# Neighbouring PSUM columns for the dense products, and transposed weight rows kept in their own slab, in a decode kernel with its backward pass

## Chip, cores and metric

One core of one Trainium2 chip. The metric is the device time of one execution in microseconds (us), median over repeated runs.

## The reference

Two layers, each an attention over a given key/value cache and a feed-forward block with squared ReLU, applied twice with the same weights to one token; then the vector-Jacobian product for one output gradient. So the kernel returns the output and the gradients of x, of both caches, and of all weights and biases. Cut to what matters:

```python
# D = 1024, 32 query heads, 4 KV heads, head size 128, cache of 65536 keys, F = 3584, all bf16
def A(x, k_cache, v_cache, wq, wo):
    q = heads(x @ wq)
    p = softmax(q @ k.T * 128 ** -0.5)          # 8 query heads share one KV head
    return merge(p @ v) @ wo

def B(x, w1, b1, w2, b2):
    r = relu(x @ w1 + b1)
    return (r * r) @ w2 + b2

x1 = x  + A(ln(x));   x2 = x1 + B(ln(x1))
x3 = x2 + A(ln(x2));  x4 = x3 + B(ln(x3))       # x4 is the output
# reference: x4 and jax.vjp(...)(grad_out)
```

## The kernel before

It makes four passes over K and V: forward of the first attention, forward of the second, backward of the second, backward of the first. Between the passes lie three "turns", chains of dense matrix-vector products: first turn wo, w1, w2, wq; second turn wo and w1 forward, w1 and wo backward; third turn wq, w2, w1 and wo backward. Products that hang on no vector of the chain run beside it while their slabs are there: w2 with the output's gradient beside the first turn's w2, and x4's own w2 product beside the third turn's. A pass is limited by its transfers; a turn is a chain of vectors, each needed by the next product.

A product whose weights are stored the right way round goes through `g_mv`: each 128x128 block is TensorE's stationary operand, and the vector's chunk is repeated over `rep` columns (64 for eight blocks, 18 for w1's 28).

```python
    def g_mv(slab_it, nk, nbk, xcol, ps_of, finish, side=None, pre=None, cols=d_cols):
        rep = 1 if ps_of is ps_bg else min(64, 512 // nbk)
        ps = ps_of([P, rep, nbk])
        ...
        for kc, slab in slab_it:
            for nb in range(nbk):
                nc.tensor.matmul(ps[:, :, nb], lhsT=cols(slab, nb), rhs=xcol(kc).to_broadcast([P, rep]), ...)
            ...
        finish(ps[:, 0, :])
```

A product with the transposed matrix goes through `Rows`. Each part (up to eight 128x128 blocks of a row of weights) is either multiplied and reduced on VectorE, or transposed on TensorE (`front`), copied from PSUM to a buffer `wt` on ScalarE or VectorE, and multiplied (`back`).

```python
        def front(self, job, kc, slab):
            ...                                   # VectorE multiply-reduce, if the balance model says so
                pt = self.ps_wt()
                for i in range(w):
                    nc.tensor.transpose(pt[:, i, :], job["cols"](slab, k0 + i), ident_b[:, :])
                ...
                wt = self.pool.tile([P, 8, P], BF, name="wt", tag="wt", bufs=self.bufs)
                evac(wt[:, 0:w, :], pt[:, 0:w, :])
                self.queue.append((job, kc, q, wt))
                if len(self.queue) >= self.bufs:
                    yield

    rows = Rows(DENSE["pool"])                    # third turn
    rows.add(PRE["wq3"], DC, R, lambda: L3["dqT"][:, gsl(lastg[2])], fin_dx2)
    def side_x4(kc, slab):
        for nb in range(DC):
            nc.tensor.matmul(ps_x4[:, :, nb], lhsT=d_cols(slab, nb), rhs=L4["gb"]..., ...)
        if kc == FC - 1:
            ...                                   # x4 = x3 + ps_x4 + b2 on VectorE
            col_to_dram(x4, D, out_0...)          # a TensorE transpose, a copy, a store
    rows.add(w2_slabs()[0], FC, DC, lambda: dx2[:], fin_dh2, mix=True, side=side_x4)
    rows.add(w1_slabs()[0], DC, FC, lambda: dh2[:], fin_dx1, cols=f_cols, mix=True)
    rows.add(wo_slabs(firstg[3])[0], R, DC, lambda: dx1[:], dO_finish(L1, firstg[3]))
    rows.run()
```

Names used below: a slab is a piece of a matrix loaded at once, a slot the memory that it takes; dqT is the last gradient of q of a pass, with which the third turn starts; dn3 and dx2 come of the wq product, dh2 of w2's, dx1 of w1's; dO (dOT in the traces) starts the next backward pass. A kc is a band of 128 rows of a matrix (28 of them in w2, four to a slab of 1 MB).

## Time and profile before

| | before |
|---|---|
| median of 3 runs | 2031.34 us (2030.72 to 2031.52) |
| span of the profiled run | 2027.6 us, mean granted TensorE clock 0.904 |
| moved by the transfers | 794.98 MB, mean 392 GB/s |
| busy: TensorE, VectorE, ScalarE | 80%, 58%, 52% of the span |

TensorE is the busiest engine on the page, and that share says little: in the passes it is busy beside transfers that run at their limit. What counts is where the transfers fall below 420 GB/s. The prediction shows these lines.

### The profile page before, as it was taken

The numbers are of one execution on the slowest core, as the hardware profiler recorded it, in microseconds if no ns is written. First come the engines' busy times: TensorE is split into PE (matmuls) and PEld (weight loads), VectorE is DVE, ScalarE is ACT, GpSimd is POOL, SyncE is SP. The second block draws the span as 40 slices with busy tenths as digits, with TensorE's granted clock in tenths as the row PEclk, the third lists the DMA queues.
The fourth block names the chain that finished last, engine by engine and source line by source line (L and its number), as shares of the span: only waits on it lengthen the run. The fifth ranks groups of instructions, "written<-read, shape, count | busy, mean of one in ns | idle before, by whom it ended". The sixth has DMA issues, their size and how long they took to land. (4 is left out here: it accounts for less than half of the span.)

```text
span 2027.6 us, 67015 instructions
## 1 busy us (share of the span) xinstructions
PE 1626.9 (80%) x30210; PEld 1332.9 (66%) x30210; DVE 1174.3 (58%) x2358; ACT 1044.6 (52%) x1613; POOL 144.5 (7%) x332
## 2 busy tenths in 40 slices
PE   6877888687877877787787887788788888698896
PEld 6877777687777776786676885455455555355554
DVE  5645455245554543544454457677667777577675
ACT  3434344144344352435363445587667667577675
POOL 0000000000000000000000001112121111111111
PEclk9989899799999987898998989889888889798888
DMA  9999999989999997899999977999999999999996
GB/s 389 420 420 420 419 423 397 371 362 420 420 418 420 420 399 279 352 420 421 420 417 412 401 267 266 370 410 423 422 420 421 393 423 396 363 402 423 421 379 245
DMA packets 110846, 794.98 MB, mean 392 GB/s; under 512 B 9425, under 2 KB 9439, under 8 KB 49375
## 3 DMA queue, kind: packets, MB, share of 16 engines
q1 hardware_dynamic: 86510, 624.99, 75.7%
q0 software_dynamic: 24048, 165.70, 19.8%
q8 instruction: 236, 3.87, 0.8%
q14 instruction: 52, 0.42, 0.1%
HBM read 624.96 MB, written 165.69 MB: 390 GB/s over the span
## 5 line engine op out<-in xcount | busy, mean ns | idle before, releaser
L153 DVE COPY kt<-ps_tr 128x1024 bf16<-128x1024 bf16 x724 | 497.8, 689 | 473.8 <-PE ps_tr L913 256.7
L150 ACT CAST arena<-ps_gg 128x1024 bf16<-128x1024 f32 x452 | 439.9, 1009 | 219.0 <-PE ps_gg L1280 160.7
L913 PE MATMUL ps_tr<-ident_b,arena 128*128 128x128 bf16 x3840 | 310.2, 226 | 60.4 <-DMA arena<-in_A_k_cache_dram 45.1
L913 PEld LDWEIGHTS <-arena 128*128 128x128 bf16 x3840 | 234.0, 101 | 66.6 <-DMA arena<-in_A_k_cache_dram 48.1
L153 DVE CAST arena<-ps_gg 128x1024 bf16<-128x1024 f32 (+1 forms) x191 | 228.9, 1198 | 82.4 <-PE ps_gg L1280 48.0
L150 ACT COPY kt<-ps_tr 128x1024 bf16<-128x1024 bf16 x164 | 172.2, 1054 | 183.9 <-PE ps_tr L1105 126.0
L1280 PE MATMUL ps_gg<-GG,xt 64*128 64x512 bf16 x1024 | 211.6, 413 | 46.4 <-DVE arena L153 26.8
L1015 PE MATMUL ps_acc<-arena 128*128 128x64 bf16 (+4 forms) x4096 | 206.0, 196 | 45.7 <-DMA arena<-in_A_v_cache_dram 31.7
L1226 PE MATMUL ps_tr<-ident_b,arena 128*128 128x128 bf16 x1824 | 175.9, 234 | 35.3 <-DMA arena<-in_A_v_cache_dram 34.4
L931 PE MATMUL ps_sc<-L_qpad,kt 128*128 128x64 bf16 (+7 forms) x3584 | 183.4, 194 | 17.9 <-issue 11.5
L996 ACT ACTIVATE arena<-S_sb,L_negm 128x128 bf16<-128x128 f32 x256 | 165.4, 1002 | 57.8 <-DVE L_negm L981 57.7
L1105 PE MATMUL ps_tr<-ident_b,arena 128*128 128x128 bf16 x1920 | 156.3, 228 | 48.3 <-DMA arena<-in_A_v_cache_dram 48.3
L1015 PEld LDWEIGHTS <-arena 128*128 128x128 bf16 x4096 | 159.8, 100 | 50.0 <-DMA arena<-in_A_v_cache_dram 34.8
L1226 PEld LDWEIGHTS <-arena 128*128 128x128 bf16 x1824 | 119.5, 104 | 88.8 <-issue 49.6
L931 PEld LDWEIGHTS <-kt 128*128 128x128 bf16 x3584 | 153.3, 100 | 23.6 <-issue 14.6
L1105 PEld LDWEIGHTS <-arena 128*128 128x128 bf16 x1920 | 118.6, 102 | 52.2 <-DMA arena<-in_A_v_cache_dram 51.0
L1306 PE MATMUL ps_acc<-X,arena 128*128 128x64 bf16 (+3 forms) x2048 | 119.7, 199 | 24.8 <-DMA arena<-in_A_k_cache_dram 24.8
L996 ACT ACTIVATION_READ_ACCUMULATOR arena<-S_sb,L_negm 128x1 f32 x256 | 127.8, 499 | 0.0
L1306 PEld LDWEIGHTS <-arena 128*128 128x128 bf16 x2048 | 87.1, 102 | 59.9 <-issue 33.1
L1150 PE MATMUL ps_acc<-dsT,arena 128*128 128x64 bf16 (+7 forms) x2048 | 103.7, 195 | 20.0 <-DMA arena<-in_A_k_cache_dram 15.8
L1280 PEld LDWEIGHTS <-xt 64*128 64x128 bf16 x1024 | 61.3, 94 | 86.3 <-issue 46.8
L1259 PE MATMUL ps_sc<-DOB,kt 128*128 128x64 bf16 (+3 forms) x1824 | 117.5, 200 | 0.0
(266 smaller groups left out, 2169.3 us busy)
## 6 DMA issues: line engine op xcount, KB each, us to landing
arena<-in_A_k_cache_dram SPq DMA_DIRECT2D x86, 2048.0 KB, 21.5
arena<-in_A_v_cache_dram SPq DMA_DIRECT2D x83, 2048.0 KB, 21.4
out_dram<-arena POOLq DMA_DIRECT2D x151, 1024.0 KB, 11.4
arena<-in_A_v_cache_dram SPq DMA_DIRECT2D x76, 1024.0 KB, 16.5
arena<-in_A_k_cache_dram SPq DMA_DIRECT2D x76, 1024.0 KB, 16.8
arena<-in_B_w_dram SPq DMA_DIRECT2D x32, 896.0 KB, 5.8
arena<-in_A_wq_dram SPq DMA_DIRECT2D x22, 1024.0 KB, 13.8
arena<-in_A_wo_dram SPq DMA_DIRECT2D x18, 1024.0 KB, 17.5
```

Source lines behind the costliest of these rows:

```text
L150: nc.scalar.copy(out=out, in_=in_)
L153: nc.vector.tensor_copy(out=out, in_=in_)
L913: nc.tensor.transpose(pt[:, i, :], kb8[:, i, :], ident_b[:, :])
L931: nc.tensor.matmul(state["ps_s"][:, s:s + w, :].rearrange("p a b -> p (a b)"), lhsT=kt[:, i, :], rhs=L["qpad"][:, g, 0:w, :].rearrange("p ...
L996: nc.scalar.activation(out=E(p, g, c0, SU)[:, :, h], in_=S[:, h, :], func=ACTF.Exp, bias=L["negm"][:, g, su, h:h + 1], scale=SCALE, accum_ ...
L1015: nc.tensor.matmul(ps_o[:, 0:w, :], lhsT=vb8[:, i, :], rhs=E(p, g, c, w), start=(c % SU == 0), stop=(c % SU == SU - 1), skip_group_check=True)
L1105: nc.tensor.transpose(pt[:, i, :], vb8[:, i, :], ident_b[:, :])
L1150: nc.tensor.matmul(ps_dq[:, 0:w, :].rearrange("p a b -> p (a b)"), lhsT=kb8[:, i, :], rhs=dsT[:, s:s + w, :].rearrange("p a b -> p (a b)") ...
L1226: nc.tensor.transpose(pt[:, i, :], vb8[:, i, :], ident_b[:, :])
L1259: nc.tensor.matmul(state["ps_dp"][:, s:s + w, :].rearrange("p a b -> p (a b)"), lhsT=vt[:, i, :], rhs=DOB[:, g, 0:w, :].rearrange("p a b - ...
L1280: nc.tensor.matmul(pg[:, 512 * h:512 * h + 512], lhsT=xt[64 * h:64 * h + 64, j1 // 8 + m, :], rhs=gg[64 * h:64 * h + 64, :, :].rearrange(" ...
L1306: nc.tensor.matmul(ps_dq[:, 0:w, :].rearrange("p a b -> p (a b)"), lhsT=kb8[:, i, :], rhs=X[:, s:s + w, :].rearrange("p a b -> p (a b)"), ...
```

## The change

Its intent: (1) PSUM columns of a product lie next to each other, (block, repeat) in place of (repeat, block); (2) wq's and wo's transposed parts are copied back into the slab that they came from, so that all eight parts can be ready before their vector arrives, in memory that needs no buffer; a slab is then freed by its last product, not by its last transpose. The diff, cut to its core:

```diff
-        ps = ps_of([P, rep, nbk])
+        ps = ps_of([P, nbk, rep])
-                nc.tensor.matmul(ps[:, :, nb], lhsT=cols(slab, nb), ...
+                nc.tensor.matmul(ps[:, nb, :], lhsT=cols(slab, nb), ...
-        finish(ps[:, 0, :])
+        finish(ps[:, :, 0])
 # Rows.front
-                if self.views:
+                sl = NOW["slab"]
+                if job["inplace"]:
+                    wt = slab[:, k0 * P:(k0 + w) * P].rearrange("p (a b) -> p a b", b=P)
+                elif self.views:
 ...
-                self.queue.append((job, kc, q, wt))
-                if len(self.queue) >= self.bufs:
+                self.queue.append((job, kc, q, wt, sl))
+                if job["inplace"]:
+                    sl.users += 1
+                else:
+                    self.parts += 1
+                if self.parts >= self.bufs:
 # Rows.back: an in-place part gives its slab up after its products; slabs() frees a slab with no users left
+            if job["inplace"]:
+                sl.users -= 1
+                if sl.over and not sl.users:
+                    sl.free()
 # Rows.run: all parts of a first in-place job go ahead of the rest
+            first = self.queue[0][0] if self.queue else None
+            while first is not None and first["inplace"] and self.queue and self.queue[0][0] is first:
+                self.back()
 # second turn (wo) and third turn (wq, wo)
-    rows.add(PRE["wq3"], DC, R, lambda: L3["dqT"][:, gsl(lastg[2])], fin_dx2)
-    ps_x4 = ps_acc([P, 64, DC])
+    rows.add(PRE["wq3"], DC, R, lambda: L3["dqT"][:, gsl(lastg[2])], fin_dx2, inplace=True)
+    ps_x4 = ps_acc([P, DC, 64])
-            nc.tensor.matmul(ps_x4[:, :, nb], ...
+            nc.tensor.matmul(ps_x4[:, nb, :], ...
-    rows.add(wo_slabs(firstg[3])[0], R, DC, lambda: dx1[:], dO_finish(L1, firstg[3]))
+    rows.add(wo_slabs(firstg[3])[0], R, DC, lambda: dx1[:], dO_finish(L1, firstg[3]), inplace=True)
```

More of the change, by code (lines that the diff above doesn't have):

```diff
@@ L289, in __init__ @@
             self.n = 2 if both else 1
+            self.users, self.over = 0, False
             self.t = wide(self.i) if both else GRAN[self.i]
@@ L432, in gen @@
                 for kk in range(kn):
+                    NOW["slab"] = sl
                     yield k + kk, v[:, kk, :]
-                sl.free()
+                sl.over = True
+                if not sl.users:
+                    sl.free()
         g = gen()
@@ L472, in g_mv @@
                 last = (kc == nk - 1) and (nb == nbk - 1)
-                nc.tensor.matmul(ps[:, :, nb], lhsT=cols(slab, nb), rhs=xcol(kc).to_broadcast([P, rep]),
+                nc.tensor.matmul(ps[:, nb, :], lhsT=cols(slab, nb), rhs=xcol(kc).to_broadcast([P, rep]),
                                  start=first, stop=last, skip_group_check=True)
@@ L567, in __init__ @@
             self.n = 0
+            self.parts = 0
             if pool is None:
@@ L576, in __init__, with add @@
             self.feed = None
-        def add(self, slab_it, nk, nj, vcol, finish, cols=d_cols, mix=False, side=None):
+        def add(self, slab_it, nk, nj, vcol, finish, cols=d_cols, mix=False, side=None, inplace=False):
             job = self.job(nk, nj, vcol, finish, cols, mix)
             job["side"] = side
+            job["inplace"] = inplace
             self.jobs.append((slab_it, job))
@@ L585, in job @@
             pieces = [(k, min(8, nj - k)) for k in range(0, nj, 8)]
-            return dict(side=None, nk=nk, pieces=pieces, nj=nj, vcol=vcol, finish=finish, done=0, cols=cols, mix=mix, vbc=vbc, slot=None)
+            return dict(side=None, inplace=False, nk=nk, pieces=pieces, nj=nj, vcol=vcol, finish=finish, done=0, cols=cols, mix=mix, vbc=vbc, slot=None)
         def begin(self, job):
@@ L649, in back @@
         def back(self):
-            job, kc, q, wt = self.queue.popleft()
+            job, kc, q, wt, sl = self.queue.popleft()
             k0, w = job["pieces"][q]
@@ L658, in back @@
                                  start=(i == 0), stop=(i == w - 1), skip_group_check=True)
+            if job["inplace"]:
+                sl.users -= 1
+                if sl.over and not sl.users:
+                    sl.free()
+            else:
+                self.parts -= 1
             self.did(job)
@@ L692, in fill @@
                 self.feed = self.fronts()
-            while len(self.queue) < self.bufs and next(self.feed, "end") != "end":
+            while self.parts < self.bufs and next(self.feed, "end") != "end":
                 pass
         def run(self):
+            self.fill()
+            first = self.queue[0][0] if self.queue else None
+            while first is not None and first["inplace"] and self.queue and self.queue[0][0] is first:
+                self.back()
             self.fill()
@@ L1508 @@
     rows.add(w1_slabs()[0], DC, FC, lambda: dh4[:], fin_dx3, cols=f_cols, mix=True)
-    rows.add(wo_slabs(firstg[2])[0], R, DC, lambda: dx3[:], dO_finish(L3, firstg[2]))
+    rows.add(wo_slabs(firstg[2])[0], R, DC, lambda: dx3[:], dO_finish(L3, firstg[2]), inplace=True)
     run(g_w1(L4, ps_mv, pre=rows.fill))
@@ L1546 @@
     rows = Rows(DENSE["pool"])
-    rows.add(PRE["wq3"], DC, R, lambda: L3["dqT"][:, gsl(lastg[2])], fin_dx2)
+    rows.add(PRE["wq3"], DC, R, lambda: L3["dqT"][:, gsl(lastg[2])], fin_dx2, inplace=True)
     x4 = vec.tile([P, DC], F32, name="x4")
-    ps_x4 = ps_acc([P, 64, DC])
+    ps_x4 = ps_acc([P, DC, 64])
     def side_x4(kc, slab):
         for nb in range(DC):
-            nc.tensor.matmul(ps_x4[:, :, nb], lhsT=d_cols(slab, nb), rhs=L4["gb"][:, kc:kc + 1].to_broadcast([P, 64]),
+            nc.tensor.matmul(ps_x4[:, nb, :], lhsT=d_cols(slab, nb), rhs=L4["gb"][:, kc:kc + 1].to_broadcast([P, 64]),
                              start=kc == 0 and nb == 0, stop=kc == FC - 1 and nb == DC - 1, skip_group_check=True)
@@ L1557, in side_x4 @@
             f = tmp.tile([P, DC], F32, name="ffn_f")
-            nc.vector.tensor_tensor(out=f[:], in0=ps_x4[:, 0, :], in1=b2c[:], op=ALU.add)
+            nc.vector.tensor_tensor(out=f[:], in0=ps_x4[:, :, 0], in1=b2c[:], op=ALU.add)
             nc.vector.tensor_tensor(out=x4[:], in0=x3[:], in1=f[:], op=ALU.add)
```

## The prediction

> **What bounds the kernel now.** I read the page first, and on it the slices of the span. The kernel makes four passes over a K and a V cache, and between them three "turns" of dense products (wo, w1, w2, wq).
>
> ```profile
> DMA  9999999989999997899999977999999999999996
> GB/s 389 420 420 420 419 423 397 371 362 420 420 418 420 420 399 279 352 420 421 420 417 412 401 267 266 370 410 423 422 420 421 393 423 396 363 402 423 421 379 245
> ```
>
> A slice is 50.7 us. Inside the passes the transfers run at 420 GB/s. The dips at slices 8 and 9, 16 and 17, and 24 to 26 are the three turns. 794.98 MB at 420 GB/s is 1893 us; the other 135 us are start, turns and tail. Compute in a pass is hidden, so only a shorter dip gains time. I then took the sums by stretch around the turns, in steps of 50 us and of 5 us.
>
> ```profile
> core 0: us, PE busy (x) PEld busy (x) DVE busy (x) ACT busy (x) POOL busy (x), PEclk, DMA share, GB/s
> 400.00:405.00 5.00, 4.62 (x89) 4.44 (x88) 5.00 (x10) 2.08 (x3) 0.00 (x0) 1.00 1.00 413
> ...
> 425.00:430.00 5.00, 4.51 (x117) 4.39 (x115) 0.36 (x2) 0.03 (x1) 0.00 (x0) 1.00 0.10 39
> ...
> 1190.00:1195.00 5.00, 5.00 (x110) 5.00 (x108) 4.85 (x9) 3.27 (x5) 0.00 (x0) 1.00 0.37 110
> ```
>
> Summing (420 - rate)/420 x 5 us over the 5 us rows, the idle transfer time is 12.6 us in the first turn (375 to 435 us), 25.1 us in the second (765 to 850) and 36.3 us in the third (1160 to 1260). In a dip the DMA queue waits for slots that the dense chain frees, so what shortens that chain shortens the dip, until the transfers are saturated again.
>
> Then the groups by shape, for the price of one dense product:
>
> ```profile
> L656 PE MATMUL ps_bg<-vcb,wt 128*128 128x64 bf16 x768 | 38.5, 197 | 6.6 <-ACT wt L150 5.2 <-DVE wt L153 0.8 <-DVE vcb L509 0.2
> L473 PE MATMUL ps_mv<-L_gb,arena 128*128 128x64 bf16 x224 | 16.6, 252 | 1.8 <-DMA arena<-in_B_w_dram 1.8
> L1553 PE MATMUL ps_acc<-L_gb,arena 128*128 128x64 bf16 x224 | 15.8, 248 | 0.0
> ```
>
> All three multiply a 128x128 block by one vector repeated over 64 columns. L656 writes neighbouring columns; L473 and L1553 write every eighth fp32. The duration contains a fixed latency, so I took the step between matmuls from the timeline:
>
> ```profile
> 369.92 1.89 PE L1015 MATMUL ps_acc<-arena 128*128 128x64 bf16 x32 [5.96 <-DMA arena<-in_A_v_cache_dram]
> 376.05 6.58 PE L473 MATMUL ps_mv<-L_oTb,arena 128*128 128x64 bf16 x64 [0.71 <-DVE L_oTb L1052]
> 778.47 4.81 PE L473 MATMUL ps_mv<-L_nb,arena 128*128 128x18 bf16 x140 [1.11 <-DVE L_nb L219]
> 423.68 3.73 PE L473 MATMUL ps_mv<-L_nb,arena 128*128 128x64 bf16 x64 [1.11 <-DVE L_nb L219]
> ```
>
> At half clock (0.50 to 0.54 granted there) neighbouring columns cost 1.8/32 = 55 ns and strided ones 6.58/64 = 103 ns. At full clock strided is 3.73/64 = 58 ns, and runs of 8 neighbouring matmuls take 0.40 to 0.44 us, 29 to 33 ns a step. The 18-column product of w1 steps at 34 ns whatever the clock or stride: another floor.
>
> Last, the wait around the third turn's first vector:
>
> ```profile
> 1173.93 0.17 DVE L1083 SCALAR_TENSOR_TENSOR L_dqT<-dqa,L_rZ 128x8 f32<-128x8 f32 x1
> 1174.19 1.01 ACT L150 COPY wt<-ps_tr 128x1024 bf16<-128x1024 bf16 x1 [13.57 <-DVE L_dqT L1083]
> 1186.02 0.15 DVE L878 TENSOR_TENSOR dn<-dn,ps_bg 128x8 f32<-128x8 f32 x1
> ```
>
> wq3's transposes sat in PSUM, but ScalarE idled 13.57 us before copying them out, until dqT was done. A copy needs no dqT: I read this as the wt buffers lying in memory that pass 3 still used (its pool closes with its last vector). From dqT to the wq product's first use is 11.9 us.
>
> **What the Trainium skill says.** "PSUM — Partial Sum Buffer", Specifications (TRN2), gives "8-byte (any non-contiguous AP slows matmuls significantly)"; the trace agrees, a factor of 1.8 to 1.9. "TensorE: Matmul & The Clock Gate", Back-to-back issue gap, gives N/1.2 ns cold and N/2.4 + 2.5 warm, 53 and 29 ns at 64 columns; the trace has 55 and 29 to 33 for neighbouring columns[...]. "HBM Reference", Specifications (TRN2), says a core streaming alone reaches about 425 GB/s; here 420, so passes have no room.
>
> **The change, part by part.** The layout turns the accumulator from (repeat, block) to (block, repeat); operands and counts stay. It touches 64 matmuls each of the first q, wo1, q3 and wo3, 224 of w2 forward and 224 of the side product x4. Their finish reads 8 values 256 bytes apart, which is nothing.
>
> *First turn.* wo1: 64 x (103 - 55) = 3.1 us, all on the path, with w1 and its loads waiting behind it. w2 forward ran from 395.3 to 420.1 us with PE at 4.5 to 5.0 us of every 5: it is PE-bound, and 224 x (58 - 30) = 6.3 us goes. But DVE was full there until 414.2, its multiply-reduces back to back from 395.4: 18.8 us, and w2's last slab landed at 411.7. Shifted by 3.1 these floors are 411.1 and 408.6 plus about 2 us of work; so w2 ends near 411.3, 8.8 us earlier. q3: 64 x (58 - 30) = 1.8 us. The chain is 10.6 us shorter. The transfers, though, have only 12.6 us of idle to give back, and part of it (375 to 390 us) only shifts: I count 9.5.
>
> *Second turn.* wo3, at half clock: 3.1 us. w1 behind it waits for slabs whose slots wo3 frees, so it all moves along. w1's rows are unchanged. In-place wo: its last two parts were transposed and copied after the vector; from vector to dO took 821.5 to 824.6 = 3.1 us, and 64 matmuls at 33 ns are 2.1: 0.9 us. Sum 4.
>
> *Third turn.* wq3: all eight parts can be copied into their own slab before dqT, in idle time. 24 transposes (2.2 us of PE) leave the path. x4: 224 x 28 ns = 6.3 us, somewhat more for the cold ones. PE was fully busy from 1174.9 to 1209 us, ending with w2's last rows, so these add: about 8.7 us. Were the wq products first in PE's queue, dx2 would come 8 us earlier; in program order six kcs of w2 (x4 and transposes) go ahead of them, then it is about 4. The end of w2's rows is PE's sum either way, near 1200.5. w1's rows shift along; in-place wo saves 0.8, limited by its slab landing at 1230.8. Sum 9.5.
>
> *Costs.* wo and wq slots come free 2 to 3 us later, after the products instead of the transposes. The transfer queue has 2 to 3 loads of 2.5 us before it then, so I count nothing. The first q lies in the first 30 us, where transfers already run at 420 from 5 us on: nothing. Pass 4's last wq keeps its own buffers: nothing.
>
> Sum 9.5 + 4 + 9.5 = 23 us. I take off some 2 us for slabs that land no earlier. 2031.3 - 21 = 2010.
>
> **The rivals.**
> 1. *Transfers hide it.* In 395 to 425 us they already run at 384 to 424 GB/s. If only shifts of the slot waits count, the first turn gives 3 to 5, and the sum is 13: 2018. Against it: the hole of 425 to 430 us (39 GB/s), which waits for the first scores and so for q3.
> 2. *DVE, ACT or the slab loads become the bound.* DVE is at 4.85 to 5.00 of 5 us beside PE in both w2 stretches. If DVE holds the third turn too, and w2's six kcs run before wq's products, that turn gives 4 to 5 instead of 9.5: 2015.
> 3. *Slots held longer.* In-place slabs delay the next loads, the queue runs dry, and in-place gives nothing or costs 1 to 3: 2013. For it: the queue already waits on slots in all three turns.
> 4. *More than I count.* If wq's products go first and the slots of w2's late slabs free earlier (the last was issued only at 1192.2 and landed about 1197), the third turn could give 12 to 14, and the sum 28: 2003.
>
> **Range and chances.** Rivals 1 to 3 together leave about 10 us of gain, rival 4 about 30. That is the range, 2000 to 2023. Over 2% would be 40.6 us, more than half of all 74 us idle in the three turns; only strong chaining would do it: 0.03. Slower by 2% has no mechanism here: 0.01.
>
> **What would show it right or wrong.** The L473 and L1553 groups of 64 columns should fall from about 250 to about 200 ns; wo1's 64 matmuls from 6.58 to about 3.5 us, w2 forward from 24.8 to about 19. ACT should not wait for dqT before copying wq3, and dqT to L878 should fall from 11.9 to 4 to 8 us. The hole before the second pass's K loads should nearly close. Pass 2 should start about 10 us earlier, pass 3 about 14, pass 4 about 23. Wrong if the 64-column step stays near 58 ns (then stride was not the cause), if pass starts move but the end does not (transfers or pass 4 absorb it), or if holes reappear where slots are held.

## The result

The changed kernel took 2015.53 us (median of 4 runs, 2012.47 to 2017.21), the kernel before in the same rounds 2031.03 (4 runs, 2024.59 to 2031.52). The ratio is 0.9929, 95% interval 0.9906 to 0.9953: the same at a margin of 2%. A ratio is the mean time of one kernel's runs over that of the other's of the same rounds, so not quite the ratio of the medians. In two later sessions the unedited changed kernel gave 2011.22 us (ratio 0.9911 [0.9894, 0.9928]) and 2011.86 us (0.9899 [0.9880, 0.9918]).

The page of the changed kernel, its transfers by slice:

```profile
DMA  9999999999999998999999986999999999999995
GB/s 389 420 419 420 419 422 399 391 406 419 420 417 419 420 404 316 371 420 420 418 413 417 394 305 254 363 404 424 421 405 404 408 419 399 358 405 424 416 377 236
```

The first dip (slices 8 and 9) rose from 371 and 362 to 391 and 406 GB/s. The second and third are still there. The sums by stretch (us, then busy time and count of PE, PEld, DVE, ACT, POOL, granted clock, DMA share, GB/s) show the same in detail:

```profile
core 0: us, PE busy (x) PEld busy (x) DVE busy (x) ACT busy (x) POOL busy (x), PEclk, DMA share, GB/s
400.00:405.00 5.00, 4.20 (x105) 4.08 (x106) 4.81 (x9) 2.90 (x4) 0.00 (x0) 1.00 1.01 418
...
425.00:430.00 5.00, 4.60 (x150) 4.55 (x151) 1.03 (x5) 2.65 (x6) 0.00 (x0) 1.00 1.01 426
...
1180.00:1185.00 5.00, 3.04 (x79) 2.88 (x77) 4.70 (x10) 3.04 (x3) 0.00 (x0) 1.00 0.68 247
```

The hole at 425 us (39 GB/s before) is gone. At 1180 us, within the third turn, TensorE now has two idle microseconds in five. Groups by shape and the first lines of the two products in the timeline:

```profile
L477 PE MATMUL ps_mv<-L_gb,arena 128*128 128x64 bf16 x224 | 11.3, 204 | 1.5 <-DMA arena<-in_B_w_dram 1.5
L1576 PE MATMUL ps_acc<-L_gb,arena 128*128 128x64 bf16 x224 | 10.1, 196 | 0.0
```

```profile
375.95 3.57 PE L477 MATMUL ps_mv<-L_oTb,arena 128*128 128x64 bf16 x64 [0.70 <-DVE L_oTb L1075]
417.14 2.15 PE L477 MATMUL ps_mv<-L_nb,arena 128*128 128x64 bf16 x64 [1.11 <-DVE L_nb L219]
...
1150.18 1.01 ACT L150 COPY arena<-ps_tr 128x1024 bf16<-128x1024 bf16 x1 [4.28 <-PE ps_tr L637]
...
1158.48 0.17 DVE L1106 SCALAR_TENSOR_TENSOR L_dqT<-dqa,L_rZ 128x8 f32<-128x8 f32 x1
...
1167.10 0.16 DVE L901 TENSOR_TENSOR dn<-dn,ps_bg 128x8 f32<-128x8 f32 x1 [1.03 <-PE ps_bg L669]
```

The mean durations fell from 252 and 248 to 204 and 196 ns; wo1's 64 matmuls from 6.58 to 3.57 us at half clock, q3's from 3.73 to 2.15 at full clock. ScalarE copies wq's parts at 1150 us, eight microseconds before dqT, in place of 13.57 us idle until it. From dqT to the end of dn3's add (L901, L878 before) it is now 8.6 us, 12.1 before.

Where the time went, by the instants of the same instructions in three profiles of each kernel (the first pair and the repeats told below), in us; the last column is the difference of the means:

| stretch | before | changed | means |
|---|---|---|---|
| first turn (last V product to q ready) | 53.5, 55.6, 52.9 | 45.4, 45.0, 45.4 | -8.7 |
| second pass | 339.3, 339.0, 339.4 | 338.7, 338.3, 339.8 | -0.3 |
| second turn (last V product to dO) | 57.9, 53.8, 54.2 | 52.9, 52.9, 52.2 | -2.7 |
| third pass (dO to dqT) | 349.3, 349.3, 349.4 | 347.6, 347.4, 348.5 | -1.5 |
| third turn (dqT to dO) | 60.8, 62.8, 60.2 | 56.0, 54.8, 54.6 | -6.1 |
| fourth pass (dO to its last dqT) | 768.4, 769.0, 774.8 | 776.1, 772.8, 770.0 | +2.3 |
| span | 2027.6, 2027.7, 2029.3 | 2015.4, 2009.4, 2009.0 | -16.9 |

Measured as in the prediction, by idle transfer time at 420 GB/s in rows of 5 us, the mean fell from 13.0 to 4.4 us in the first turn (375 to 435 us), from 23.1 to 18.9 in the second (here 755 to 850) and from 40.3 to 35.2 in the third (here 1140 to 1260, as the turn now begins earlier).

The first comparison alone would have told a different story: second turn -5.0, fourth pass +7.8. So the questions for the experiments were: why the third turn gave 5 to 6 us and not 9.5, which part gave what, and whether the fourth pass really pays something back.

### The profile page after: what moved, and what is told of

It reads as the page before. It is cut to its first block, busy times and chain, and to the rows that moved or that the text cites. A ratio compares the mean times of both kernels' runs of the same rounds, so it can differ in the third digit from the quotient of the medians.

```text
span 2015.4 us, 67001 instructions
## 1 busy us (share of the span) xinstructions
PE 1613.8 (80%) x30210; PEld 1315.4 (65%) x30210; DVE 1175.3 (58%) x2358; ACT 1043.6 (52%) x1613; POOL 144.4 (7%) x332
## 3 DMA queue, kind: packets, MB, share of 16 engines
q8 instruction: 236, 3.87, 0.8%
## 5 line engine op out<-in xcount | busy, mean ns | idle before, releaser
L936 PE MATMUL ps_tr<-ident_b,arena 128*128 128x128 bf16 x3840 | 311.3, 226 | 55.7 <-DMA arena<-in_A_k_cache_dram 41.4
```

The lines of the kernel that those rows point to most:

```text
L936: nc.tensor.transpose(pt[:, i, :], kb8[:, i, :], ident_b[:, :])
```

## The experiments

My theory at first: in the third turn VectorE's multiply-reduces are the bound once dx2 is there. The rival: the sum of TensorE's work, as predicted.

### Layout alone

```diff
-    ... fin_dx2, inplace=True)     # and both wo products
+    ... fin_dx2)
```

> The changed kernel without the in-place transposes: only the layout of the PSUM columns is new. All theories: the first turn as in the changed kernel (second pass begins 8 to 9 us earlier than before), wo3 3 us, so the third pass begins 11 to 13 us earlier (13.7 with both parts). Third turn. My theory (VectorE's multiply-reduces and the tail after them bound it once dx2 is there): x4's shorter matmuls gain little, so dx2 to dh2 goes from 21.7 us before to about 20, and dqT to dn3 stays near 12; the turn gains 1 to 2.5 us. Rival (TensorE's sum bounds it): dqT to dh2 falls by the whole 6 us of x4, from 35.5 to about 29.5. Fourth pass (dO to its last dqT, 768.4 us before, 776.1 after): if the loss of 7.8 us comes from slots held in place, it is 767 to 770 here; if it is noise of the transfers, anything from 766 to 778. Time by my theory 2031 - 13 - 1 = about 2016 if the fourth pass loses nothing; 2024 if it loses 8 as well.

Measured: 2019.76 us (5 runs, 2017.89 to 2020.68), ratio 0.9954 [0.9942, 0.9966]. First turn 45.1 us, the whole gain there. Second turn 52.3. Third turn 59.7, only 1.6 us under the mean of before; dqT to dn3 11.0, dqT to dh2 33.4. Fourth pass 772.8. ScalarE waits for dqT again, so the idle time before the copies belongs to the missing in-place buffers and not to the layout:

```profile
1159.22 0.17 DVE L1106 SCALAR_TENSOR_TENSOR L_dqT<-dqa,L_rZ 128x8 f32<-128x8 f32 x1
1159.47 1.01 ACT L150 COPY wt<-ps_tr 128x1024 bf16<-128x1024 bf16 x1 [13.46 <-DVE L_dqT L1106]
```

The time landed between the two given. In the profiled run the fourth pass was 2 us above the mean of the kernel before; whether that is why isn't shown. The third pass began 14.9 us earlier than in the first profile of before, more than the 11 to 13 expected.

### In place alone

```diff
-        ps = ps_of([P, nbk, rep])
+        ps = ps_of([P, rep, nbk])      # matmul, finish and x4 likewise
```

> The changed kernel with every layout strided again: only the in-place transposes of wo and wq are new. First turn and the start of the second pass: as before, within 1 us. Second turn: my theory says in place gains nothing there (its second slab lands only as the vector arrives): dx3 to dO 3.5 +- 0.3 us, against 2.6 if the prediction's 0.9 us is real. Third turn: dqT to dn3 falls from 12.1 to 8 to 9.5 us by both theories (ScalarE no longer waits); dx2 to dh2: VectorE-bound, 20 to 22 us, and the turn gains 2 to 4; bounded by TensorE's sum, only the 2 us of transposes are gained at dh2 and dx2 to dh2 rises to 23. Fourth pass: if the slots held in place cost it 8 us, it is 775 to 778, and the time is 2032 to 2036, no gain at all; otherwise 768 +- 3 and 2027 to 2029.

Measured: 2023.14 us (6 runs, 2018.63 to 2030.62), ratio 0.9972 [0.9956, 0.9988]. First turn 54.1 us, as before. dx3 to dO 3.8: no gain by wo. Third turn 55.7, 5.6 us under the mean of before, more than the 2 to 4 expected. dqT to dn3 was 8.0 us and dqT to dh2 30.9, but at a granted clock of 1.00 throughout, where the kernel before had 0.72 to 0.75 in its first 12 us; how much of the gain is the clock's, this run does not tell. Fourth pass 770.9 us, below the 775 to 778 that a cost of slots held in place asks for. The time was below both ranges given, 2027 to 2029 and 2032 to 2036.

The two parts add up: 0.46% and 0.28% against 0.71 to 1.01% for both. The layout is worth its time in the first turn, in place in the third.

### x4 alone strided again

```diff
-    ps_x4 = ps_acc([P, DC, 64])
+    ps_x4 = ps_acc([P, 64, DC])        # matmul and add likewise
```

> The changed kernel with x4's 224 matmuls alone strided again (58 instead of 30 ns a step, 6.3 us of TensorE in the third turn); the order of instructions is the same. My theory (VectorE bounds the third turn from dx2 on, TensorE had 3 us of slack in five there): dqT to dh2 grows from 30.6 us by 1 to 2.5 us, dqT to dn3 by about 1 (six of x4's blocks of 8 matmuls lie ahead of wq's second half), x4 itself is done late. Prediction's step (TensorE's sum): it grows by 5.5 to 6.5 us. Time against the changed kernel: +1 to +2.5 us by mine, about +6 by the rival, if the fourth pass is alike.

Measured: 2012.51 us (4 runs, 2011.11 to 2013.06), ratio 0.9919 [0.9906, 0.9932]. dqT to dh2 32.2 us against 30.6 in the first profile of the changed kernel: +1.6, as my theory had it, and far from the 5.5 to 6.5 of the rival. The clock was not quite alike (0.83 granted from dqT to dn3 here, 0.74 there). In-place alone against the changed kernel's repeat, told below, both at 1.00, gives 30.9 against 28.8: +2.1. Between dx2 and dh2 the clock was 1.00 in every kernel, so that stretch compares cleanly. Before, this one and the changed kernel, each from its own dx2 to its own dh2, columns as above:

```profile
1188.07:1209.57 21.50, 21.49 (x438) 21.04 (x436) 16.26 (x37) 14.20 (x16) 0.80 (x3) 1.00 0.67 234
```

```profile
1171.96:1192.60 20.64, 20.54 (x423) 20.27 (x421) 16.26 (x36) 13.99 (x16) 0.80 (x3) 1.00 0.87 320
```

```profile
1169.15:1189.11 19.96, 17.57 (x416) 16.93 (x417) 16.11 (x36) 14.11 (x16) 0.80 (x3) 1.00 0.91 339
```

With x4 strided TensorE is busy 20.54 of 20.64 us: its sum is the bound, just as the prediction read it. With neighbouring columns it is busy 17.57 of 19.96. Of 3.0 us saved, 2.3 turned into idle time.

### wq's products first

```diff
+            with tc.high_priority():
                 while first is not None and first["inplace"] and ...:
                     self.back()
```

> The changed kernel, with wq's (and wo's) products of an in-place job at a higher priority: wq3's 64 matmuls stand in one block in TensorE's queue, ahead of the six blocks of x4 and transposes of w2 which the changed kernel has between its two halves. Mean to show what the third turn is bound by. Chained on the vector (my theory: multiply-reduces start when dx2 is there, then VectorE or the tail bounds): dqT to dn3 falls from 8.6 to about 4 to 5 us, dx2 about 3.5 to 4 us earlier, dh2 and the next dO about 3 us earlier, time -3 us if the fourth pass is alike. TensorE's sum: dx2 earlier, but dh2 at the same time within 0.7 us, and no gain. Slots of wq come free 3 us earlier here, so if holding them costs the fourth pass something, that shrinks too.

Measured: 2008.09 us (4 runs, 2006.85 to 2009.95), ratio 0.9901 [0.9887, 0.9916]. dqT to dn3 3.6 us (8.6, 6.8 and 6.8 in the three profiles of the changed kernel), so dx2 came 3 to 5 us earlier. But dqT to dh2 was 29.5 us, inside the 28.8 to 30.6 of the changed kernel: dx2 to dh2 grew from 20.0 to 23.6. My theory, that the chain hangs on dx2 and VectorE, fell here: work that had stood ahead of wq now stands behind it. What holds is TensorE's order: its sum and the waits met in it. For one of them, 1.7 us amid eight transposes, the views name no releaser ("issue"):

```profile
1178.67 0.22 PE L637 MATMUL ps_sc<-ident_b,arena 128*128 128x128 bf16 x1
1180.59 0.55 PE L637 MATMUL ps_sc<-ident_b,arena 128*128 128x128 bf16 x7 [1.70 <-issue]
```

The packed traces show what it is. I counted TensorE's weight loads and matmuls in order. Between dqT and dh2 the 14 profiles hold 14 such stops of over 0.3 us, and before each of them the count is a whole number of 256s plus the same 193; this holds too for the last kernel told below, whose added matmuls shift all that follow. Before each stop ended, 1.2 to 1.5 us earlier, a packet of 16384 bytes had landed on the queue of the page's line

```profile
q8 instruction: 236, 3.87, 0.8%
```

and TensorE's 60443 instructions in 236 packets are 256 in each. So I read these stops as waits for TensorE's own instructions. Over a whole execution all stops of over 0.3 us without a releaser, 47 to 62 of them and 44 to 59 us together, lie at such a count (193 or 194). No run changes them on purpose.

### What TensorE did from dqT to dh2

I summed the steps between starts of consecutive matmuls by kind, for the whole way from dqT to dh2; "rest" is the interval less these. All in us.

| | x4 | transposes | Rows products | other | rest | interval |
|---|---|---|---|---|---|---|
| before | 12.4 | 14.2 | 7.1 | 1.0 | 0.8 | 35.5 |
| x4 strided | 12.4 | 11.3 | 7.1 | 1.0 | 0.3 | 32.0 |
| changed, first profile | 7.6 | 11.3 | 7.1 | 1.0 | 3.5 | 30.5 |
| changed, repeat | 7.2 | 10.1 | 6.3 | 1.0 | 4.0 | 28.6 |

Transposes lost 2.9 us (24 of them now before dqT), x4 4.8. Of these 7.7 us 2.7 came back as waits. (The clocks differ: 0.72 to 0.83 granted up to dn3 in the first three rows, 1.00 in the last.) The waits of the changed kernel there, and what VectorE did at that time:

```profile
PE ps_mv L190 <- DVE x L1582: 2.0, 1, 2.0
PE ps_bg L669 <- DVE vcb L513: 0.9, 1, 0.9
```

```profile
1183.23 1.22 DVE L628 SCALAR_TENSOR_TENSOR mv_junk<-arena,vbc 128x1024 bf16<-128x1024 bf16 x1
...
1184.37 0.16 DVE L1581 TENSOR_TENSOR ffn_f<-ps_acc,b2c 128x8 f32<-128x8 f32 x1
1184.57 0.17 DVE L1582 TENSOR_TENSOR x<-x,ffn_f 128x8 f32<-128x8 f32 x1
```

The 2.0 us are the transpose of x4 for its output (L190). It stands in the middle of TensorE's order, waits for x4's add, and that add stands behind eleven multiply-reduces of 1.15 us each on VectorE. "TensorE: Matmul & The Clock Gate", Architectural detail, of the Trainium skill says that ScalarE and VectorE take their instructions strictly in order; the add, whose PSUM input was complete at about 1182, agrees with it. Nothing on the chain needs x4: it is an output. So the wait can be taken out of the way. In the repeats of the changed kernel the wait was 0.8 and 0.4 us, after a stop for instructions of 1.2 and 1.5 in place of 0.4; x4's transpose began 15.64 us after dx2 in all three. With wq first it waited for nothing.

### x4's output late

```diff
     def fin_dx1(y):
         ...
+        x4_out()                       # the add, the transpose and the store of x4
-        if kc == FC - 1:
-            ...                        # taken out of side_x4
```

> The changed kernel with x4's last add and its output moved from the middle of the third turn to behind dx1, so that no TensorE instruction waits there for VectorE, which has 12 multiply-reduces queued ahead of that add. In the changed kernel TensorE stood 2.0 us before the transpose of x4 while work for it lay behind. Theory now (TensorE's own order bounds the turn: its sum plus the waits in it): dqT to dh2 falls by 1.3 to 2.0 us, from 30.6 to about 28.6 to 29.3, dO 1.3 to 2 us earlier against dqT. Rival (VectorE bounds it): the wait only moves, dqT to dh2 within 0.5 us of 30.6. Time -1.5 us against the repeat by the first, 0 by the second; below the noise of one run, so the milestones decide.

Measured: 2010.92 us (4 runs, 2007.72 to 2011.10), ratio 0.9904 [0.9889, 0.9919]; the repeat of the changed kernel beside it 2011.22. dqT to dh2 27.7 us, below all three of the changed kernel (30.6, 28.8, 28.8). From dx2 to dh2 it is 18.49 us, where the changed kernel has 19.96 in each of three profiles:

```profile
1168.52:1187.01 18.49, 17.39 (x415) 16.82 (x416) 15.84 (x35) 14.09 (x16) 0.14 (x2) 1.00 0.92 348
```

VectorE's multiply-reduces are the same, so VectorE's sum was not the bound; its order, seen through TensorE's wait, was. 1.5 us came and not 2.0: stops for instructions, 0.60 and 0.44 us, which the wait for x4 had covered, are now on the way. 18.49 less these is 17.45; the last kernel below, which also has x4 late, took 18.90 with stops of 0.61 and 0.84, and that less these is 17.45 too. The 28.6 to 29.3 expected for dqT to dh2 was reckoned from the cold first profile; against the repeats it fell by 1.1. In time the step is below what these runs resolve; the second turn, which this edit leaves alone, took 55.0 us here and 52.2 to 52.9 in the changed kernel.

### Late output and wq first

> x4's output late, and wq's products in one block ahead of x4's blocks. TensorE's order as theory: wq first moves dx2 about 5 us earlier, but TensorE's work up to dh2 is the same 27 us, so dqT to dh2 is 28.0 to 29.3, about the same as with the late output alone, and less than the 29.5 of wq first alone only if the 2.2 us in which TensorE stood for no shown reason there are gone. VectorE as bound: chained on dx2, dqT to dh2 about 26 to 27. Time 2006 to 2009, the best so far or level with wq first alone.

The edit is the high-priority block above, put into the late-output kernel. Measured: 2013.19 us (5 runs, 2004.96 to 2013.94), ratio 0.9905 [0.9888, 0.9923]. dqT to dh2 29.9 us, neither of the two ranges: the stop for instructions was 2.2 us here, in the same place, and the granted clock in the first 4 us was 0.50. The time was above the 2006 to 2009 expected. From dx2 to dh2 it was 23.75 us against 23.62 with wq first alone, where x4's transpose had not waited: with no wait to take away, the late output brings nothing, and neither does the order alone.

### wo through its buffers again

```diff
-    rows.add(wo_slabs(firstg[2])[0], ..., inplace=True)   # and the one of the third turn
+    rows.add(wo_slabs(firstg[2])[0], ...)
```

> The changed kernel with wq3 in place and both wo products of turns two and three through their buffers again. If wo in place is worth what was predicted, dx3 to dO grows from 3.7 by 0.9 us and dx1 to dO from 3.4 by 0.8; if its late landing had eaten that (my reading), dx3 to dO stays 3.5 to 3.7 and dx1 to dO 3.4 to 3.7. Time within 1 us of the repeat either way. Its slots are freed as before by wo, so the fourth pass tells once more whether slots matter: 766 to 773 if they do not.

Measured: 2015.20 us (4 runs, 2012.86 to 2017.19), ratio 0.9924 [0.9911, 0.9938]; beside it the changed kernel's 0.9911 [0.9894, 0.9928], not told apart, though the medians lie 4.0 us apart where 1 was expected. dx3 to dO 3.50 us, dx1 to dO 3.66, both as expected. The changed kernel had 3.71, 3.75 and 2.99, the kernel before 3.50, 3.87 and 3.84; from dx1 it was 3.36, 3.73 and 3.72 against 3.67, 3.50 and 3.50. So wo in place clearly gave something in one of these six cases. Of the six other kernels with wo in place, three (wq first, both, and the last one below) had 2.98 or 2.99 from dx3 to dO, the other three 3.69 to 3.83; from dx1 they had 2.98 to 3.52, and 3.96 in one. What decides it in the profiles that I read is in the second turn's timeline, the changed kernel's first profile, then this one's:

```profile
806.95 1.07 PE L637 MATMUL ps_sc<-ident_b,arena 128*128 128x128 bf16 x16 [0.57 <-DMA arena<-in_A_wo_dram]
807.85 1.06 PE L637 MATMUL ps_tr<-ident_b,arena 128*128 128x128 bf16 x16
808.74 2.15 PE L669 MATMUL ps_bg<-vcb,arena 128*128 128x64 bf16 x64
```

```profile
808.59 0.41 PE L669 MATMUL ps_bg<-vcb,wt 128*128 128x64 bf16 x8 [0.36 <-DVE vcb L513]
...
809.98 1.66 PE L669 MATMUL ps_bg<-vcb,wt 128*128 128x64 bf16 x48
```

In the changed kernel TensorE waits 0.57 us for the second wo slab, which lands at 806.95, 0.4 us before dx3 is there (807.39). Its four parts are transposed first, and the 64 products begin only at 808.74. Through buffers TensorE waits 0.36 us for the vector and then does transposes and products by turns, which comes to the same. In the profile with 2.99 us the same 32 transposes began at 807.36, and dx3 came at 808.52: with the slab 1.2 us ahead in place of 0.4 the gain is there.

### The kernels again, unedited

> The changed kernel once more, unedited, on the chip that the next three share: how much of its fourth pass (776.1 us from dO to the last dqT in its first profile, 768.4 before, 767.6 to 772.8 in the four variants) is noise. If noise: 766 to 773 here and a median time of 2009 to 2014, since two variants that do no better in the turns gave 2012.5 and 2008.1. If the in-place slots cost pass 4 its 8 us in this kernel alone: 774 to 778 again, 2015 to 2017. The third turn should repeat: dqT to dh2 30.6 +- 0.7 us.

> The changed kernel a third time. First turn 45 to 46, second 52.5 to 53.5, third 54.5 to 56, by the clock after dqT: 28.7 to 29 us from dqT to dh2 if it is 1.00 there, 30.5 if it is below 0.8. Fourth pass 768 to 775. Median time 2009 to 2015.

> The kernel before once more, one look. What it can tell: the length of the fourth pass (768.4 us in its first profile; 767.6 to 776.1 in nine profiles of the changed kernel and its variants). If that pass is noise, 768 to 775 here and the 7.8 us which the first comparison lost there are mostly the luck of one profile; if the change really costs it, 766 to 769. And the granted clock at the starts of the turns: wo1 at 0.54 took 8.5 us, wo3 at 0.59 took 8.3; where the clock is 1.00 I expect wo3 at 5.5, and the second turn 3 us shorter than its 57.9.

> The kernel before a second time, for the same two questions: fourth pass 768 to 775 if noise, 766 to 769 if the change costs it. First turn 53.5 +- 1, second 54.5 to 58 by the clock of wo3, third 58.5 to 61 by the clock after dqT.

Measured: the changed kernel 2011.22 us (5 runs, 2007.85 to 2018.42) and 2011.86 (6 runs, 2008.19 to 2017.07); the kernel before 2029.51 and 2031.07. The first repeat missed what was expected of its third turn, 30.6 +- 0.7 us from dqT to dh2: it took 28.8. Two things came out.

First, the fourth pass: 768.4, 769.0 and 774.8 us before; 776.1, 772.8 and 770.0 changed; 767.6 to 773.5 in the other eight kernels, nearly all of which also hold slots in place. The lengths overlap. The 7.8 us of the first comparison were mostly that pair of profiles; a real cost of up to about 2 us is neither shown nor excluded.

Second, the granted clock where a turn begins differs from run to run of one program. The 64 matmuls of wo3, the first profile of before, then its repeat; then the last repeat of the changed kernel:

```profile
768.58 6.58 PE L473 MATMUL ps_mv<-L_oTb,arena 128*128 128x64 bf16 x64 [0.70 <-DVE L_oTb L1052]
```

```profile
770.36 3.73 PE L473 MATMUL ps_mv<-L_oTb,arena 128*128 128x64 bf16 x64 [0.70 <-DVE L_oTb L1052]
```

```profile
761.03 2.15 PE L477 MATMUL ps_mv<-L_oTb,arena 128*128 128x64 bf16 x64 [0.71 <-DVE L_oTb L1075]
```

So the first profile of before was a cold one, of low granted clock, in the second turn (0.59 granted over wo3), and its two repeats are 3.7 to 4.1 us shorter there. After dqT, the changed kernel had 0.74 granted in its first profile and 1.00 in both repeats: dqT to dn3 took 8.6 and then 6.8 us (8.45 and 6.60 to the start of the add). "TensorE: Matmul & The Clock Gate", What's actually happening, says that the clock follows a free-running window of about 3.4 us of activity, so that the count of cold matmuls varies between runs of one kernel; these pairs agree. In the four profiles with wq through buffers the clock was 0.50 from 1.7 us before dqT to 4 us after it; in seven of the ten with wq in place, one of them with matmuls added for that, it was 1.00 before dqT, and in five it stayed so. So part of what in place gains in the third turn may be the clock; no run separates them.

Not every cold start costs: in the first turn wo1's 64 matmuls took 3.57 us in one profile of the changed kernel and 2.15 in another, and w1 after them ended at the same time within 0.1 us, since it waits for its slabs. Nor does the stride there, at full clock: the second repeat of before, with 3.73 us for wo1, ended w1 at 391.1 us, where the changed kernel's three profiles ended it at 390.9 to 391.1 and the two other profiles of before at 393.6 and 394.0.

### Keeping TensorE busy before dqT

```diff
+            if (g, c8) == items[-4]:
+                keep_busy(36)          # matmuls of the identity, never read
             ...
+            if (g, c8) == items[-1]:
+                keep_busy(20)
```

> x4's output late, and 56 matmuls that no one reads, put where TensorE waits at the end of the third pass: 36 ahead of the last four K tiles' products (it waited 1.4 us for that slab) and 20 behind them (0.9 us until the vector). Question: does an idle TensorE there cost the third turn its clock? In two profiles of the same changed kernel dqT to dn3 took 8.45 us at a granted clock of 0.74 and 6.60 at 1.00. If idling is the cause: 1.00 from dqT on, dqT to dn3 6.5 to 7.0, dqT to dh2 27.4 to 28, third turn 52.5 to 53.5 us. Rival (the clock falls by something else than TensorE's idling): about 0.7 in the first 8 us, dqT to dn3 8 to 9, and the matmuls in between cost up to 1 us more. Time -2 us against the changed kernel's median if the first, 0 to +1 if the second.

Measured: 2009.04 us (5 runs, 2007.07 to 2011.66), ratio 0.9888 [0.9868, 0.9907]; the changed kernel beside it 0.9899 [0.9880, 0.9918]. The clock was 1.00 from dqT on, but so it was in both repeats without these matmuls; one profile does not tell the two theories apart. dqT to dn3 was 7.2 us, above the 6.5 to 7.0, with a stop of 0.41 us for instructions amid wq's products. The third turn took 55.1 us, so the 52.5 to 53.5 expected was missed: dqT to dh2 was 28.3, and 1 us more went between dh2 and dx1 than in the late-output kernel. Inconclusive. It does repeat the late output's effect: dx2 to dh2 18.9 us against 19.96.

No version is shown to beat the changed kernel in time: wq first (0.9901), late output (0.9904) and this one (0.9888) all lie within the interval of its repeats. A late output of x4 is the only edit whose gain is shown, in its own stretch.

## Why the prediction was right or wrong

The class and the range were right: 2010 us predicted, 2000 to 2023; measured 2015.53 and, repeated, 2011.22 and 2011.86. The working behind it was right in the mechanism and wrong in some sizes, which partly cancelled, so that a repeat within 2 us of 2010 is in part luck. The second, third and fourth passes began 8.8, 11.8 and 19.4 us earlier in the means, for about 10, 14 and 23 predicted. One reading of the prediction is off without consequence: its rows from 1160 to 1260 us sum to 38.7 us of idle transfers, not 36.3.

- **The price of a strided column**: right. The step fell from 103 to 56 ns cold (3.57 us for 64) and from 58 to 34 ns warm (2.15 us), wo1 gave 3.11 us for 3.1 predicted in the first pair. The 30 ns put in for q3 and x4 were too few: 34 came, so q3 gave 1.6 us at full clock for 1.8, and x4 4.8 on TensorE for 6.3. w1's 18-column product did not change: 7.78 us for 224 matmuls, 34.7 ns, after 34 before.
- **First turn, 9.5 us**: nearly right, 8.7, but with two terms wrong. "3.1 us, all on the path" for wo1 took the half clock of one profile for a property of the kernel: 2.5 of it were left at w1's end in the first pair, and against the repeat of before with a warm wo1 nothing. w2 forward, "8.8 us earlier", ended 6.8 us earlier in the first pair: it took 20.9 us, not "about 19". Its last slab landed at 408.97, near the floor of 408.6 given, but 64 of its 224 matmuls were still to come, 32 of them of the slab before, so that slab was not the bound. TensorE, busy without a pause from 409.4 us on, rather was: its sum, and 1.9 us of waits for ScalarE's copies. The hole before the second pass closed as foretold.
- **Second turn, 4 us**: the first comparison's 5.0 looked like a hit, but more than half of it was the clock. With the clock at 1.00 over wo3 on both sides (two repeats of before, the last of the changed kernel) the turn went from 54.0 to 52.2: 1.8 us. The step "wo3, at half clock: 3.1 us" took the clock of one profile for a property of the kernel; warm, 3.73 - 2.15 = 1.6 us is all there is. "In-place wo" with 0.9 us failed in two profiles of three: the slab lands so shortly before the vector that its transposes stay on the path. In the third, with the slab 1.2 us ahead, it held.
- **Third turn, 9.5 us**: 6.1, the largest miss; with the low clock after dqT on both sides (first profile of the changed kernel) 5.3. The failing step is "PE was fully busy from 1174.9 to 1209 us, ending with w2's last rows, so these add: about 8.7 us". The wq part of it held: 2.9 us of transposes left the path for 2.2 predicted, ScalarE no longer waited for dqT, and dqT to dn3 fell into the 4 to 8 predicted where the clock was full (6.8, 6.8) and to 8.6 where it was not. x4 failed: its matmuls shrank by 4.8 us on TensorE, but strided against neighbouring x4 moved dh2 by only 1.6 us (2.1 at clock 1.00). TensorE's sum was the bound before, and ceased to be it some 2 us into the saving; then its wait for x4's add behind VectorE's queue took over. That is rival 2 by its name, and its 4 to 5 us were nearer than my 9.5, but by a wait in program order: moving that add alone gave 1.5 us back. wo's 0.8 us did not come.
- **Passes "shift along"**: the third pass is 1.5 us shorter, which nobody predicted. It is 349.3 to 349.5 us in four profiles with wq through buffers and 346.1 to 348.9 in all ten with wq in place. The traces show where: the last K slab of the pass landed 346.9 to 347.1 us after dO in the four, 344.4 to 346.7 in the ten, and from there to dqT it took 2.39 us where the clock was 0.50 and 1.72 where it was 1.00. I did not test why the slab came earlier; it stays open. The fourth pass is not shown to differ.
- **Slots held longer (rival 3)**: not shown. Neither the time nor the fourth pass told wo in place from wo through buffers.
- **The sum, 23 us**: less the shortfalls of 0.8, 1.3 and 3.4 us in the turns, less 2.3 in the fourth pass, plus 1.8 in the second and third, is 17.0; the means of the spans differ by 16.9. That these agree was to be expected, since both come of the same instants; whether the 2 us taken off for late slabs are among the shortfalls, it does not tell.

## What to carry to other kernels

Before adding up savings on an engine that is busy all through a stretch, look in its order for the instruction that waits for another engine; it will be the bound as soon as the sum has shrunk to it, and an output that nobody on the chain needs should not stand there. Ask of a prefetch whether the vector or the slab arrives last: transposing ahead helps only in the first case. Where an engine stops and the views name no releaser, count its instructions up to there. And take a second profile of the kernel before, because one profile's granted clock, or the length of one long pass, can be worth as much as the change.

## What the Trainium skill lacked or had wrong

- "PSUM — Partial Sum Buffer", Specifications (TRN2), says that a non-contiguous pattern slows matmuls "significantly", without a figure. Here 64 fp32 columns 32 bytes apart took 58 ns a matmul against 34 ns for neighbouring ones (64 in 3.73 and 2.15 us) at full clock, and 103 against 56 ns at 0.54 and 0.50 granted. It does not say when the stride is free: 18 columns at 112 bytes apart took 34 ns, and 34.7 ns when neighbouring.
- "TensorE: Matmul & The Clock Gate", Back-to-back issue gap, gives about 81 ns for a stream of weight load and 128-column matmul. Here 181 such pairs (the transposes from dqT to dh2 in the changed kernel's repeat, clock 1.00) took 10.09 us, 55.7 ns each; the page's lower figure for an isolated gap fits this stream.
- "Runtime: NRT & Kernel Launch", Instruction fetch mechanics, has no figure for what crossing from one block of instructions to the next can cost. In the 14 profiles here TensorE stopped for 0.4 to 2.2 us at 14 such crossings between dqT and dh2, as long as the effects studied here, and for 44 to 59 us in stops of over 0.3 us in a whole execution.
